# Sliding-window attention and gated MLP: where the x^T of batches 3 to 7 is transposed, and when batch 3's scores start

## The chip, the cores and the metric

The kernel runs on one core of one Trainium2 chip. The metric is the device time of one execution in microseconds (us). Executions of one and the same kernel scatter by about one per cent here, so medians of several runs are given, and effects of less than a microsecond are read from the lengths of single stages in the profile.

## The reference, cut to what matters

```python
# attention: q, k, v are (8 batches, 8 heads, 576 positions, 64)
scores = (q @ k^T) / 8;  masked to 0 <= i - j < 64
attn   = softmax(scores);  out = attn @ v
# x: (4608 tokens, 512), the heads of a token side by side
h = x @ w_in                      # (4608, 2048)
g = h * clip(h + 3, 0, 6) / 6
return (g @ w_out)                # (4608, 512), float32
```

## The kernel before

The MLP goes in nine stages of 512 tokens (0 to 8). A stage has two halves: `s1` makes 16 chunks of the hidden layer, each of four 128x512 matmuls, and `s2` makes four output tiles in four quarters each, again four matmuls per quarter. So a stage has 128 large matmuls on TensorE (PE). The attention of a later batch is woven between them as *pieces*: stage 1 computes batch 2, stage 2 batch 3, and so on to stage 6 with batch 7. `p1` lists the pieces after each chunk of `s1`, `p2` those after each quarter of `s2`.

A batch has four pairs of heads. For each pair, `SS` makes the scores (PE), the exponentials (ScalarE, ACT) and the mask (VectorE, DVE); `N_` makes PV on PE and normalizes on DVE; then the result has to be transposed, to become x^T, the right operand of the next stages. That is done either by PE and a copy (`X_`), or by a DMA transpose (`xt_dma`), which the sync engine's queue (SP) issues.

```python
def xt_pe(bt, g, tr):                       # X_ calls it
    opg = opgs.pop((bt.b, g))
    for qb in range(KB):                    # KB = 5
        nc.tensor.transpose(out=tr[:, qb * P : (qb + 1) * P], in_=..., identity=ident[:])
    return lambda: acopy(out=xT[:, g, bt.b * S : (bt.b + 1) * S], in_=tr[:, 0:S])

def xt_dma(bt, g):
    ...
    nc.sync.dma_start_transpose(out=xT[:, g, t0 : t0 + SP].rearrange(...), in_=opg[:]...)

def pieces(bt):
    ...                                     # batch 2: all by X_
    p1 = {10: [f(SS, 0)], 14: [f(SS, 1)]}   # batches 3 to 7
    p2 = {
        0: [f(SS, 2)], 1: [f(N_, 0)], 3: [f(SS, 3), f(xt_dma, 0)], 4: [f(N_, 1)],
        6: [f(xt_dma, 1)], 7: [f(N_, 2)], 9: [f(xt_dma, 2)], 10: [f(N_, 3)], 12: [f(X_, 3)],
    }
    return p1, p2
...
for T in range(1, NTB):
    p1, p2 = pieces(nxt)
    b = T + 2
    if b < B:
        sts, _ = load_for_dma(b)            # 15 loads of q, k, v on SP
        nxt = Batch(b)
        p1.setdefault(12 if T == 1 else 6, []).append(...cast_for_dma(sts))   # POOL
        p2.setdefault(6 if T == 1 else 12, []).append(...transpose_by_dma())  # QT, KT, on SP
    stage_(T, None, p1, p2)
```

The same SP queue thus carries, in program order, the loads of the batch after next, its QT and KT transposes (SBUF to SBUF), the x^T transposes of the current batch, and the output tiles.

The softmax here doesn't subtract the row's maximum and nothing guards it: scores larger than these inputs give would overflow.

Of the kernel before, what the change touches and what calls it, by code (L numbers as in the profile page):

```python
# [24 lines left out]
def kernel(  # L25
# [98 lines left out]
    def load_for_dma(b):  # L124
        sts, ins = [], []
        for n, src in (("qst", q), ("kst", k), ("vst", v)):
            t = stage.tile([P, KB, H, D], F32, name=n, tag=n)
            ins += load_blocks(t, src, b, range(KB), SR if src is v else 0)
            sts.append(t)
        return tuple(sts), ins  # L130
# [446 lines left out]
    bt, st = Batch(0), stage0  # L577
# [77 lines left out]
    bt, st = Batch(1), st1  # L655
# [56 lines left out]
    def stage_(T, bt, pieces1, pieces2):  # L712
        if T == 1:
            m = s1(1, ((0, 1), (2,)))
            run(m, 1)
            X_(Batch(1), NG - 1)
            run(m, 1)
        else:
            m = s1(T)
        for i in range(NFC):  # L720
            run(m, 1)
            for f in pieces1.get(i, ()):
                f()
        m = s2(T, BY_BLOCK)
        for i in range(16):
            run(m, 1)
            for f in pieces2.get(i, ()):
                f()

    def pieces(bt):  # L730
        if bt is None:
            return {}, {}
        f = lambda fn, *a: lambda: fn(bt, *a)
        p1, p2 = {}, {}
        if bt.b == 2:
            return p1, {
                0: [f(SS, 0)], 1: [f(SS, 1)], 3: [f(N_, 0), f(SS, 2)], 5: [f(X_, 0)],
                6: [f(N_, 1), f(SS, 3)], 8: [f(X_, 1)], 9: [f(N_, 2)], 11: [f(X_, 2)],
                12: [f(N_, 3)], 14: [f(X_, 3)],
            }  # L740
        p1 = {10: [f(SS, 0)], 14: [f(SS, 1)]}
        p2 = {
            0: [f(SS, 2)], 1: [f(N_, 0)], 3: [f(SS, 3), f(xt_dma, 0)], 4: [f(N_, 1)],
            6: [f(xt_dma, 1)], 7: [f(N_, 2)], 9: [f(xt_dma, 2)], 10: [f(N_, 3)], 12: [f(X_, 3)],
        }
        return p1, p2

# [6 lines left out]
    nxt, pend = bt2, None  # L754
# [3 lines that stand above are left out]
        nxt = None  # L758
        if b < B:
            sts, _ = load_for_dma(b)  # L760
            nxt = Batch(b)
            p1.setdefault(12 if T == 1 else 6, []).append(
                lambda bt=nxt, sts=sts: bt.cast_for_dma(sts)
            )
            p2.setdefault(6 if T == 1 else 12, []).append(lambda bt=nxt: bt.transpose_by_dma())
        stage_(T, None, p1, p2)


# [28 lines left out]
```

## Time and profile before

| what | kernel before |
|---|---|
| median of the first runs | 319.6 us |
| span of the profile | 317.6 us |
| PE busy | 300.8 us (95%) |
| ACT, DVE busy | 56%, 55% |
| stage 2 with stage 3 | 67.3 us |
| stages 4, 5, 6 | 32.03, 32.04, 32.04 us |
| stage 7 (no attention in it) | 27.6 us |

A stage is measured here from the first large matmul of its `s1` that the profile shows to that of the next stage. Some matmul records are missing from some profiles. If the first matmul of stage 3 is one of them, its row counts 7 and not 8. Stage 2 then reads too long, and stage 3 reads 0.22 us too short; sums over both are right. The first lines of the profile page of the kernel before:

```profile
span 317.6 us, 5604 instructions
PE 300.8 (95%) x2131; PEld 149.5 (47%) x2167; DVE 173.9 (55%) x331; ACT 177.9 (56%) x265; POOL 85.7 (27%) x131
```

PE is the engine that bounds the kernel. In the steady stages there is no idle time on it to speak of. The busy times by stretch of the kernel before, for stages 2 and 3 together and then for stages 4 and 5 (columns: stretch, length, busy time of each engine with its instruction count, granted PE clock, DMA share, GB/s):

```profile
95.06:162.37 67.31, 63.72 (x467) 31.74 (x475) 38.98 (x72) 38.58 (x58) 25.50 (x34) 1.00 1.17 220
162.37:194.40 32.03, 31.82 (x234) 15.85 (x237) 19.72 (x36) 19.17 (x29) 9.71 (x13) 1.00 1.04 203
194.40:226.44 32.04, 31.83 (x235) 15.87 (x237) 19.93 (x36) 19.17 (x29) 10.27 (x13) 1.00 1.02 201
```

Stages 4 to 6 have 0.2 us of idle time each; stages 2 and 3 have 3.6 us in 67.3. The waits of PE from stage 2 to the end of stage 6, in the kernel before (engine, line, what it waited for: total us, times, longest):

```profile
PE st L347 <- DMA KT<-kn: 2.0, 1, 2.0
PE st L466 <- DMA xT<-opg: 1.0, 1, 1.0
```

The PE timeline of the kernel before shows where these are: the first scores of batch 3 wait for KT, and stage 3 waits for x^T after its first matmuls. (The last bracket is the idle time before the instruction and what ended it.)

```profile
103.69 1.03 PE L466 MATMUL hT<-xT,win 128*128 128x512 bf16 x4
106.69 0.51 PE L347 MATMUL st<-QT,KT 64*128 64x192 bf16 x10 [1.97 <-DMA KT<-kn]
...
126.26 0.44 PE L407 MATMUL hT<-ident,opg 128*128 128x128 bf16 x5
126.54 2.54 PE L503 MATMUL acc<-wout,gT 128*128 128x512 bf16 x11
129.13 0.59 PE L466 MATMUL st<-xT,win 128*128 128x512 bf16 x2
130.77 1.46 PE L466 MATMUL st<-xT,win 128*128 128x512 bf16 x6 [1.04 <-DMA xT<-opg]
```

The row with `ident` is one x^T by PE: five transposes, and 0.28 us later the next matmul issues. The SP queue of the kernel before in the same stage (start, duration of issuing, what):

```profile
102.24 2.75 SPq L266 DMA_TRANSPOSE KT<-kn  x1
...
106.64 4.92 SPq L94 DMA_DIRECT2D qst<-in_q_dram  x5
111.61 5.39 SPq L94 DMA_DIRECT2D kst<-in_k_dram  x5
117.10 6.92 SPq L94 DMA_DIRECT2D vst<-in_v_dram  x5
...
124.78 2.60 SPq L418 DMA_TRANSPOSE xT<-opg  x2
127.48 0.53 SPq L512 DMA_DIRECT2D out_dram<-osb  x1
128.11 1.24 SPq L418 DMA_TRANSPOSE xT<-opg  x1
```

The lines left out are output tiles; the queue has no gap over 0.1 us from 102 to 129 us. The x^T transposes stand behind fifteen loads.

### The profile page before, as it was taken

The numbers are of one execution on the slowest core, as the hardware profiler recorded it, in microseconds if no ns is written. First come the engines' busy times: TensorE is split into PE (matmuls) and PEld (weight loads), VectorE is DVE, ScalarE is ACT, GpSimd is POOL, SyncE is SP. The second block draws the span as 40 slices with busy tenths as digits, with TensorE's granted clock in tenths as the row PEclk, the third lists the DMA queues.
The fourth block names the chain that finished last, engine by engine and source line by source line (L and its number), as shares of the span: only waits on it lengthen the run. The fifth ranks groups of instructions, "written<-read, shape, count | busy, mean of one in ns | idle before, by whom it ended". The sixth has DMA issues, their size and how long they took to land.

```text
span 317.6 us, 5604 instructions
## 1 busy us (share of the span) xinstructions
PE 300.8 (95%) x2131; PEld 149.5 (47%) x2167; DVE 173.9 (55%) x331; ACT 177.9 (56%) x265; POOL 85.7 (27%) x131
## 2 busy tenths in 40 slices
PE   8989799999999799899999999999999999999995
PEld 3454345544554355344544554445444544444442
DVE  4658643476636665277527853785378438406700
ACT  2748753387637771487258725872587347417711
POOL 5741805363045143305610650065000000000000
PEclk9999999999999999999999999999999999999999
DMA  8999999999799999999999998999800630010011
GB/s 211 237 173 253 238 199 205 204 184 248 158 208 209 270 215 205 191 254 204 195 257 210 207 184 208 211 201 185 204 34 2 122 75 0 28 73 33 0 68 66
DMA packets 150843, 52.64 MB, mean 166 GB/s; under 512 B 138272, under 2 KB 146464, under 8 KB 150816
## 3 DMA queue, kind: packets, MB, share of 16 engines
q1 hardware_dynamic: 146000, 46.77, 72.7%
q0 software_dynamic: 4544, 5.24, 9.5%
q8 instruction: 17, 0.28, 0.4%
q10 hardware_dynamic: 272, 0.26, 0.2%
q14 instruction: 10, 0.08, 0.1%
HBM read 36.70 MB, written 9.44 MB: 145 GB/s over the span
## 4 chain that ended last, share of the span: by engine, by line
PE 63%; DMA 21%; SPq 8%; POOL 3%; issue 2%; DVE 1%; ACT 1%; POOLq 0%
PE o L503 15%; PE acc L503 14%; PE hT L466 14%; PE acc L466 5%; PE o L466 5%; SPq L94 5%; DMA vst<-in_v_dram 4%; DMA kst<-in_k_dram 4%; DMA KT<-kn 4%; DMA qst<-in_q_dram 3%; PE st L466 3%; PE st L347 3%; DMA wout<-in_moe_w_out_dram 3%; DMA win<-in_moe_w_in_dram 3%; PE hT L377 1%
## 5 line engine op out<-in xcount | busy, mean ns | idle before, releaser
L466 PEld LDWEIGHTS <-win 128*128 128x128 bf16 x576 | 55.3, 98 | 67.2 <-issue 2.3
L503 PEld LDWEIGHTS <-gT 128*128 128x128 bf16 x576 | 52.9, 98 | 57.5 <-issue 0.6
L503 PE MATMUL o<-wout,gT 128*128 128x512 bf16 x274 | 67.5, 379 | 1.5 <-DMA wout<-in_moe_w_out_dram 0.7
L503 PE MATMUL acc<-wout,gT 128*128 128x512 bf16 x278 | 67.1, 379 | 0.7 <-issue 0.3
L466 PE MATMUL hT<-xT,win 128*128 128x512 bf16 x266 | 65.7, 379 | 0.3
L355 ACT ACTIVATE pT<-st 128x768 bf16<-128x768 f32 x64 | 48.9, 813 | 10.8 <-PE st L347 10.7
L473 ACT ACTIVATE t<-hT,half 128x512 bf16<-128x512 f32 x68 | 46.7, 690 | 9.6 <-PE hT L466 9.2
L474 DVE SCALAR_TENSOR_TENSOR gT<-t,hT 128x512 bf16<-128x512 bf16 x68 | 46.4, 685 | 9.4 <-ACT t L473 9.1
L474 DVE SCALAR_TENSOR_TENSOR gT<-t,st 128x512 bf16<-128x512 bf16 (+1 forms) x26 | 19.7, 768 | 52.9 <-ACT t L473 52.9
L365 DVE TENSOR_TENSOR pT<-pT,mask 128x1536 bf16<-128x1536 bf16 x28 | 28.1, 1004 | 23.0 <-ACT pT L355 23.0
L509 ACT COPY osb<-o 128x512 f32<-128x512 f32 x18 | 10.6, 586 | 46.2 <-PE o L503 46.2
L252 POOL CAST qn<-qst 128x512 bf16<-128x512 f32 x24 | 16.1, 712 | 74.1 <-DMA qst<-in_q_dram 59.7
L509 ACT COPY osb<-acc 128x512 f32<-128x512 f32 x18 | 10.6, 587 | 35.7 <-PE acc L503 33.7
L466 PE MATMUL st<-xT,win 128*128 128x512 bf16 x117 | 28.2, 379 | 1.7 <-DMA xT<-opg 1.0
L397 DVE TENSOR_TENSOR opg<-hT,rec 128x320 bf16<-128x320 f32 x56 | 27.5, 492 | 1.9
L466 PE MATMUL acc<-xT,win 128*128 128x512 bf16 x91 | 23.6, 379 | 0.1
L466 PE MATMUL o<-xT,win 128*128 128x512 bf16 x90 | 23.5, 379 | 0.1
L473 ACT ACTIVATE t<-st,half 128x512 bf16<-128x512 f32 (+1 forms) x26 | 19.4, 752 | 7.2 <-PE st L466 7.1
L377 PEld LDWEIGHTS <-pT 128*128 128x128 bf16 x256 | 17.8, 97 | 9.1 <-issue 1.4
L347 PE MATMUL st<-QT,KT 64*128 64x192 bf16 (+2 forms) x320 | 17.9, 229 | 4.2 <-DMA KT<-kn 2.4
L394 DVE RECIPROCAL rec<-hT 128x5 f32<-128x5 f32 x56 | 10.5, 188 | 20.0 <-PE hT L386 19.9
L243 POOL CAST V<-vst 128x512 bf16<-128x512 f32 (+1 forms) x14 | 16.4, 1168 | 17.4 <-DMA vst<-in_v_dram 17.0
(76 smaller groups left out, 269.2 us busy)
## 6 DMA issues: line engine op xcount, KB each, us to landing
out_dram<-osb SPq DMA_DIRECT2D x32, 256.0 KB, 2.4
qst<-in_q_dram SPq DMA_DIRECT2D x28, 256.0 KB, 4.7
kst<-in_k_dram SPq DMA_DIRECT2D x27, 256.0 KB, 5.4
vst<-in_v_dram SPq DMA_DIRECT2D x24, 256.0 KB, 5.1
vst<-in_v_dram SPq DMA_DIRECT2D x24, 128.0 KB, 4.1
win<-in_moe_w_in_dram POOLq DMA_DIRECT2D x4, 512.0 KB, 7.6
wout<-in_moe_w_out_dram POOLq DMA_DIRECT2D x4, 512.0 KB, 8.8
qst<-in_q_dram SPq DMA_DIRECT2D x2, 512.0 KB, 6.1
```

What stands on the lines that cost most here:

```text
L243: copy(out=self.V[:, 0 : KB - 1, h0:h1, 0:D], in_=vst[:, 0 : KB - 1, h0:h1, :])
L252: pcopy(out=n[:, g, 0 : KB - 1, :, :].rearrange("p k h d -> p k (h d)"), in_=s[:, 0 : KB - 1, 2 * g : 2 * g + 2, :].rearrange("p k h d -> ...
L347: nc.tensor.matmul(st[:, h, o0 : o0 + n], lhsT=bt.KT[h * D : (h + 1) * D, g, k0 : k0 + P], rhs=bt.QT[h * D : (h + 1) * D, g, q0 : q0 + n], ...
L355: nc.scalar.activation(out=pT[:, :, 2 * u : 2 * u + 2, 0:QW], in_=st[:, :, 0:w].rearrange("p h (k w) -> p h k w", k=2), func=EXP, scale=scale,
L365: nc.vector.tensor_tensor(out=pT[:, :, :, 0:QW], in0=pT[:, :, :, 0:QW], in1=mask[:].rearrange("p (h k) w -> p h k w", h=2), op=MULT,)
L377: nc.tensor.matmul(ob, lhsT=pT[:, h, qb, 0:P], rhs=V[:, qb, 2 * g + h, :], start=True, stop=(qb == 0),)
L397: nc.vector.tensor_tensor(out=opgs[bt.b, g][:, :, h, :], in0=ov[:, :, 0:D], in1=rec[:].unsqueeze(2).to_broadcast([P, KB, D]), op=MULT,)
L466: nc.tensor.matmul(hT, lhsT=win16[:, g, fc * P : (fc + 1) * P], rhs=xT[:, g, t0 : t0 + TB], start=(g == 0), stop=(g == NG - 1),)
L473: nc.scalar.activation(out=t1[:], in_=hT, func=RELU, bias=half[:], scale=1.0 / 6.0)
L474: nc.vector.scalar_tensor_tensor(out=out, in0=t1[:], scalar=1.0, in1=hT, op0=MIN, op1=MULT,)
L503: nc.tensor.matmul(accs[ts], lhsT=gT[:, fc, ts * P : (ts + 1) * P], rhs=wout16[:, fc, :], start=(fc == 0), stop=(fc == NFC - 1),)
L509: nc.scalar.copy(out=osb[:], in_=accs[ts])
```

## The change

Its intent: batch 3 asks for KT later and takes all its x^T by PE, since SP is late in stage 2; from batch 4 on, the fourth x^T goes by DMA too, which takes the transposes off PE, and PV is moved up so that the last DMA is in time. The QT/KT transposes of batch 4 move from quarter 12 of stage 2 to quarter 6.

```diff
+        if bt.b == 3:
+            return {13: [f(SS, 0)]}, {
+                0: [f(SS, 1)], 3: [f(N_, 0), f(SS, 2)], 5: [f(X_, 0)], 6: [f(N_, 1), f(SS, 3)],
+                8: [f(X_, 1)], 9: [f(N_, 2)], 11: [f(X_, 2)], 12: [f(N_, 3)], 14: [f(X_, 3)],
+            }
-        p1 = {10: [f(SS, 0)], 14: [f(SS, 1)]}
+        p1 = {10: [f(SS, 0)], 13: [f(SS, 1)]}
         p2 = {
-            0: [f(SS, 2)], 1: [f(N_, 0)], 3: [f(SS, 3), f(xt_dma, 0)], 4: [f(N_, 1)],
-            6: [f(xt_dma, 1)], 7: [f(N_, 2)], 9: [f(xt_dma, 2)], 10: [f(N_, 3)], 12: [f(X_, 3)],
+            0: [f(SS, 2)], 1: [f(N_, 0)], 2: [f(SS, 3)], 3: [f(N_, 1), f(xt_dma, 0)],
+            5: [f(xt_dma, 1)], 6: [f(N_, 2)], 8: [f(N_, 3), f(xt_dma, 2)], 10: [f(xt_dma, 3)],
         }
...
-            p2.setdefault(6 if T == 1 else 12, []).append(lambda bt=nxt: bt.transpose_by_dma())
+            p2.setdefault(6 if T < 3 else 12, []).append(lambda bt=nxt: bt.transpose_by_dma())
```

## The prediction

> **What bounds the kernel now.** TensorE: PE is busy 300.8 us of 317.6 (95%), ACT 56%, DVE 55%; granted clock 1.00 throughout. In the timeline 128x512 matmuls issue every 0.216 us, so a pure stage of 128 takes 27.6 us (stages 7, 8). An attention stage adds four pairs of scores (0.44 us each), eight PV heads (0.25 us each) and one x^T by PE (0.28 us for five transposes): about 31.7; stages 4 to 6 take 32.0 to 32.2. The idle time is in stage 2 (batch 3): the waits view has PE on KT<-kn for 2.4 us, the longest 1.97 us at 104.7 to 106.7 (pair 0 of batch 3, asked after chunk 10); and 1.04 us on xT<-opg at the start of stage 3. There SP's queue is late: the loads of batch 4 occupy it to 124.0, and the third x^T transpose issues at 128.1, landing 2.6 us later.
>
> **What the change does.**
> 1. Batch 3's scores start three chunks (2.6 us) later. KT landed at 106.6; PE will ask at about 107.2. Saves 1.97 us, with half a microsecond of slack.
> 2. Batch 3's x^T all by PE: +15 transposes, 3 x 0.28 = +0.84 us. The last copy is placed as in stage 1, after which stage 2 began without a wait. Removes the 1.04 us wait.
> 3. Batch 4's QT/KT transposes move ahead in SP's queue, so stage 3's loads start near 132 rather than 137 us. Off PE's path; slack only.
> 4. Batches 4 to 7: the fourth x^T by DMA. PE 4 x -0.28 = -1.12 us. SP gets one 1.24 us issue more per stage. In stage 5 its loads end at 214.8 and its QT transpose starts at 223.9, so it fits. Last x^T issued near 221.4, landing (median 2.9 us) near 224.3, before the next stage at 226.1: no wait.
> 5. PV one or two quarters earlier: worth nothing to PE, needed for 4. Its price: PV of pair 1 asks for its PSUM bank 2.8 us after PV of pair 0, before which DVE must mask pair 2 and do four small instructions. With the mask at 0.96 us that just fits; in stages 4 and 5 one took 1.36 us as a POOL cast started beside it. The Trainium skill ("SBUF — State Buffer", on the shared port pair) says that DVE and GpSimd exclude each other there; the trace agrees in that instruction. I allow 0 to 0.35 us a stage, +0.4 in all.
>
> The skill ("TensorE: Matmul & The Clock Gate", Part 4) gives about 275 ns for a 128x128 PE transpose in a kernel; here five in a row hold PE up only 0.28 us together, which I use. So net PE work falls only 0.28 us.
>
> **Sum.** -1.97 - 1.04 + 0.84 - 1.12 + 0.4 = -2.9 us: 319.6 becomes 316.7 (range 315.5 to 318.2), 0.9% faster, all on PE's chain, most of it in stage 2 and at stage 3's start. Chances: faster by over 2% 0.02, within 2% 0.96, slower 0.02.
>
> **What would show it.** 1: no wait over 0.3 us on KT in stage 2. 2: none on xT at stage 3's start, which comes near 127.9 instead of 129.1. 3: stage 3's loads begin by 133. 4: stages 3 to 6 take 31.7 to 32.0 us; 16 x^T transposes by DMA, the fourth landing over 1 us before the next stage. 5: small idle times of PE before PV of pair 1, on DVE.
>
> **What would make it wrong.** KT landing later than before (DMA engines are nearly full in stage 2); the fourth transpose queued behind late loads on SP, giving 1 us or more of wait at four stage starts (then 319 to 320); PV stalls in every stage, larger than allowed.

## The result

The changed kernel took 316.08 us (median; 314.71 to 316.42 over four runs; a fifth took 316.84), the kernel before 319.67 us in the same rounds. The ratio is 0.9887 (95% interval 0.9849 to 0.9926): 1.1% faster. Ratios here and below are the mean time of one kernel's fast runs over that of the other's of the same rounds, so they are not quite the ratio of the medians quoted. Two repeats in later sessions gave 0.9892 and 0.9889.

The span of the changed kernel's profile is 4.7 us shorter, but 1.3 us of that lie before stage 2 (which began at 93.75 instead of 95.06 us), where the change touches nothing. Its repeats began stage 2 at 96.10 and 95.06 us, so this part is scatter. What belongs to the change is the stretch from stage 2 to the end of stage 6: 163.42 us before, 160.00 after (160.26 and 161.11 in the two later profiles of the changed kernel; the last of them has a wait of 0.76 us, see below). The page of the changed kernel and the same three stretches:

```profile
span 312.9 us, 5589 instructions
PE 298.8 (96%) x2126; PEld 149.0 (48%) x2162; DVE 174.5 (56%) x331; ACT 177.2 (57%) x264; POOL 86.1 (28%) x131
```

```profile
93.75:158.37 64.62, 64.04 (x476) 32.54 (x484) 39.38 (x72) 39.94 (x60) 25.77 (x34) 1.00 1.15 220
158.37:190.13 31.76, 31.55 (x230) 15.60 (x233) 19.94 (x36) 18.52 (x28) 10.25 (x13) 1.00 1.03 214
190.13:222.00 31.87, 31.66 (x230) 15.64 (x233) 19.78 (x36) 18.51 (x28) 10.32 (x13) 1.00 1.11 207
```

Stages 2 and 3 became 2.7 us shorter although PE is busy 0.3 us longer there, and stages 4 to 6 became 0.27, 0.17 and 0.29 us shorter with PE less busy by the same amount. The PE timeline of the changed kernel, at the places where the kernel before waited:

```profile
105.94 0.51 PE L347 MATMUL st<-QT,KT 64*128 64x192 bf16 x10
...
126.84 1.67 PE L466 MATMUL st<-xT,win 128*128 128x512 bf16 x7
```

Neither row has a bracket: both waits are gone. And the SP queue of the changed kernel in stages 2 and 3:

```profile
100.87 2.80 SPq L266 DMA_TRANSPOSE KT<-kn  x1
...
123.11 3.54 SPq L266 DMA_TRANSPOSE QT<-qn  x1
126.75 3.74 SPq L266 DMA_TRANSPOSE KT<-kn  x1
...
132.14 4.95 SPq L94 DMA_DIRECT2D qst<-in_q_dram  x5
...
150.28 2.60 SPq L418 DMA_TRANSPOSE xT<-opg  x2
...
153.60 2.56 SPq L418 DMA_TRANSPOSE xT<-opg  x2
```

The loads of stage 3 begin at 132.1 us instead of 137.0 (38.4 us after the start of stage 2 instead of 41.9), and all four x^T of batch 4 are issued by 156.2 us. The last one starts at 154.9 and lands 2.6 us later, at 157.5, before stage 4 begins at 158.4.

### The profile page after: what moved, and what is told of

It is laid out like the page before. It is cut to its first block, busy times and chain, and to the rows that moved or that the text cites. A ratio compares the mean times of both kernels' runs of the same rounds, so it can differ in the third digit from the quotient of the medians.

```text
span 312.9 us, 5589 instructions
## 1 busy us (share of the span) xinstructions
PE 298.8 (96%) x2126; PEld 149.0 (48%) x2162; DVE 174.5 (56%) x331; ACT 177.2 (57%) x264; POOL 86.1 (28%) x131
## 4 chain that ended last, share of the span: by engine, by line
PE 88%; ACT 3%; DMA 3%; SPq 2%; DVE 1%; issue 1%; POOL 1%
PE o L503 20%; PE acc L503 19%; PE hT L466 18%; PE st L466 8%; PE acc L466 6%; PE o L466 6%; PE st L347 4%; PE hT L377 2%; PE hT L382 2%; DMA qst<-in_q_dram 1%; PE hT L407 1%; DMA vst<-in_v_dram 1%; ACT pT L355 1%; DVE gT L474 1%; SPq L82 1%
## 5 line engine op out<-in xcount | busy, mean ns | idle before, releaser
L503 PE MATMUL acc<-wout,gT 128*128 128x512 bf16 x275 | 66.1, 379 | 0.8 <-issue 0.2
L466 PE MATMUL hT<-xT,win 128*128 128x512 bf16 x267 | 64.9, 379 | 0.3
```

What stands on the lines that cost most here:

```text
L466: nc.tensor.matmul(hT, lhsT=win16[:, g, fc * P : (fc + 1) * P], rhs=xT[:, g, t0 : t0 + TB], start=(g == 0), stop=(g == NG - 1),)
L503: nc.tensor.matmul(accs[ts], lhsT=gT[:, fc, ts * P : (ts + 1) * P], rhs=wout16[:, fc, :], start=(fc == 0), stop=(fc == NFC - 1),)
```

## The experiments

The sum in the prediction treats the two waits as separate items. A rival reading is that they stand one behind the other on SP: the x^T transposes come when the loads are through, so if PE arrives earlier because one wait is gone, it only waits longer at the next. To tell them apart, the two parts of batch 3 were tried alone. All four kernels of this first set have the new schedule for batches 4 to 7, and ran on one chip.

| kernel | scores of batch 3 | x^T of batch 3 | median us | ratio to before (95%) | stages 2+3, us | waits of PE in stages 2 to 6 |
|---|---|---|---|---|---|---|
| only_b4on | after chunk 10 | 3 DMA, 1 PE | 318.23 | 0.9947 (0.9915 to 0.9979) | 69.09 | KT 3.0 |
| b3_by_dma | after chunk 13 | 3 DMA, 1 PE | 318.31 | 0.9954 (0.9921 to 0.9986) | 67.08 | xT 2.8 |
| scores_early | after chunk 10 | PE | 318.89 | 0.9962 (0.9928 to 0.9997) | 66.88 | KT 2.1 |
| after_again | after chunk 13 | PE | 316.77 | 0.9892 (0.9856 to 0.9927) | 64.80 | none |

The kernel before had a median of 320.21 us in these rounds.

### Batches 4 to 7 alone: only_b4on

```diff
# against the changed kernel: batch 3 and the place of QT/KT as in the kernel before
-            return {13: [f(SS, 0)]}, { ...all by X_... }
+            p1 = {10: [f(SS, 0)], 14: [f(SS, 1)]}
+            p2 = { ...as in the kernel before, xt_dma 0 to 2, X_ 3... }
```

> Batch 3 as in the kernel before, batches 4 to 7 as in the change. My sum: only the four x^T transposes of 0.28 us leave TensorE, so about 1.0 us off before (ratio about 0.997); stages 4 to 6 take about 31.8 us instead of 32.0; both waits of batch 3 are still there: about 2 us on KT in stage 2 (a little more or less with the moment the transpose lands) and about 1 us on xT at the start of stage 3. Rival: most of the gain of the whole change comes from these batches (ratio 0.991 or less).

Measured: the ratio is 0.9947, about where the sum puts it (0.997 is inside the interval), and stages 5 and 6 take 31.76 and 31.75 us; stage 4 takes 32.06, for a reason given under step 5 below. The profiled execution was slower than the others of this kernel (319.57 us, clock 0.995 over the span) and shows something that was not expected. The wait on KT was 2.96 us instead of 1.97, and the matmuls after it ran at half speed. The PE timeline of only_b4on:

```profile
106.40 0.51 PE L347 MATMUL st<-QT,KT 64*128 64x192 bf16 x10 [2.96 <-DMA KT<-kn]
106.84 1.54 PE L466 MATMUL hT<-xT,win 128*128 128x512 bf16 x4
108.18 1.91 PE L466 MATMUL o<-xT,win 128*128 128x512 bf16 x4
109.88 1.41 PE L466 MATMUL acc<-xT,win 128*128 128x512 bf16 x4
```

Four matmuls that take 0.86 us from one row to the next elsewhere took 1.70 us from 108.18 to 109.88. The busy times of only_b4on in the stretches 106 to 111 and 111 to 116 us confirm that it is the clock (the third number from the end):

```profile
106.00:111.00 5.00, 4.60 (x22) 1.98 (x23) 1.71 (x3) 2.89 (x4) 0.00 (x0) 0.66 1.14 271
111.00:116.00 5.00, 5.00 (x46) 2.45 (x45) 3.60 (x5) 4.50 (x7) 1.79 (x2) 1.00 1.35 211
```

Stage 2 lasted 37.2 us in this execution. PE reached stage 3 so late, at 130.95 us, that x^T had landed, and the second wait does not appear. This is taken up again below.

### The late scores alone: b3_by_dma

```diff
# against the changed kernel (QT/KT of batch 4 also back after quarter 12)
             return {13: [f(SS, 0)]}, {
-                0: [f(SS, 1)], 3: [f(N_, 0), f(SS, 2)], 5: [f(X_, 0)], 6: [f(N_, 1), f(SS, 3)],
-                8: [f(X_, 1)], 9: [f(N_, 2)], 11: [f(X_, 2)], 12: [f(N_, 3)], 14: [f(X_, 3)],
+                0: [f(SS, 1)], 3: [f(N_, 0), f(SS, 2)], 5: [f(xt_dma, 0)], 6: [f(N_, 1), f(SS, 3), f(xt_dma, 1)],
+                9: [f(N_, 2)], 10: [f(xt_dma, 2)], 12: [f(N_, 3)], 14: [f(X_, 3)],
```

> As only_b4on, but batch 3's scores three chunks later; its x^T still by DMA for three pairs, QT/KT of batch 4 in the old place. Independent-waits theory (as my prediction adds them up): the KT wait of about 2 us goes and the xT wait stays at about 1 us, so 2 us faster than only_b4on. Series theory: the start of stage 3 is set by the SP queue (loads of batch 4 until about 29 us after the start of stage 2, then the x^T transposes in a row), which does not move when TensorE arrives earlier; the KT wait goes and the xT wait grows to 2.5 to 3.5 us; the same time as only_b4on within 0.5 us.

Measured: the wait on KT is gone, and the wait on x^T grew from 1.04 to 2.8 us. The time is that of only_b4on. The PE timeline of b3_by_dma at the start of stage 3:

```profile
128.04 0.38 PE L466 MATMUL st<-xT,win 128*128 128x512 bf16 x1 [1.51 <-DMA xT<-opg]
128.58 0.38 PE L466 MATMUL st<-xT,win 128*128 128x512 bf16 x1 [0.16 <-DMA xT<-opg]
130.08 1.46 PE L466 MATMUL st<-xT,win 128*128 128x512 bf16 x6 [1.12 <-DMA xT<-opg]
```

PE now waits for each of the three transposes in turn. Its third x^T was issued at 127.30 us, 33.0 us after the start of stage 2, as in the kernel before (128.11, 33.1 us after). The stretch of stages 2 and 3 is 67.08 us against 67.31 before, and 0.28 of that is the fourth x^T of batch 4 that left PE in stage 3. So the late scores alone gained nothing: the wait of 1.97 us came back at the next place where PE meets the SP queue. The series theory holds, and the items of the sum are not independent. No run put the x^T transposes ahead of the loads in SP's queue, which would be another way to have them earlier.

### The x^T by PE alone: scores_early

```diff
-            return {13: [f(SS, 0)]}, {
+            return {10: [f(SS, 0)]}, {
```

> The changed kernel, but batch 3's first scores after chunk 10 as before; its x^T by PE. Both theories: a wait on KT of about 2 us comes back in stage 2, no wait on xT at the start of stage 3, about 2 us slower than the changed kernel. If the KT wait were not the reason, it would be as fast as the changed kernel.

Measured: a wait on KT of 2.08 us in stage 2, no wait on x^T, and 318.89 us against 316.77 of the changed kernel on the same chip. Stage 2 is 35.0 us, 2.1 us more than in the changed kernel on the same chip (32.87 in after_again). The PE timeline of scores_early:

```profile
105.54 0.51 PE L347 MATMUL st<-QT,KT 64*128 64x192 bf16 x10 [2.08 <-DMA KT<-kn]
```

So the wait is worth its full length once nothing from SP stands behind it.

### The changed kernel again: after_again

> The changed kernel again, as the comparison for the three others on this chip. Ratio to before about 0.989 (3 to 4 us less). Its stage 2 begins within 0.5 us of where the kernel before has it if the 1.3 us that its first profile began stage 2 earlier was chance; if it begins 1.3 us earlier again, the change does something to the stages before it that I do not know of.

Measured: 316.77 us, ratio 0.9892. Stage 2 began at 96.10 us, 1.0 us later than in the kernel before (0.5 was expected at most) and not earlier again, so the early start in the first profile was chance. This execution had a wait on KT of 0.84 us in stage 1 (batch 2) and none in stage 2.

### Batch 3 alone: only_b3

```diff
-        p1 = {10: [f(SS, 0)], 13: [f(SS, 1)]}
-        p2 = { ...four xt_dma... }
+        p1 = {10: [f(SS, 0)], 14: [f(SS, 1)]}
+        p2 = { ...as in the kernel before... }
```

> Batch 3 as in the change (late scores, x^T by PE, QT/KT of batch 4 earlier), batches 4 to 7 as before. My sum: -1.97 (KT) -1.04 (xT) +0.84 (15 transposes) = about 2.2 us off before, ratio about 0.993; stages 4 to 6 take 32.0 us as before. Rival: under 1 us.

This and the next three ran on another chip of the same kind, where the kernel before had a median of 320.31 us (318.75 to 323.33) and the scatter was larger. Measured: 318.89 us, ratio 0.9946 (0.9896 to 0.9995). Stage 2 reads 33.08 us, and stages 3 to 6 32.03, 32.04, 32.03 and 32.03 us: from stage 2 to the end of stage 6 161.21 us, 2.2 less than before, as the sum says.

### The fourth x^T back on PE: fourth_pe

```diff
-            ...10: [f(xt_dma, 3)],
+            ...10: [f(X_, 3)],
```

> The changed kernel, but the fourth x^T of batches 4 to 7 on TensorE again, in the same place (PV still moved up). My sum: 4 x 0.28 = about 1.1 us slower than the changed kernel, plus what TensorE waits for DVE before the transposes (they come two quarters after PV of pair 3: none expected). Stages 4 to 6 about 32.1 us.

Measured: 317.66 us (median of five fast runs and one slow one of 322.93), ratio of the fast runs 0.9913. Stages 4 to 6 took 32.03, 32.32 and 32.03 us; from stage 2 to the end of stage 6 161.28 us, 1.3 us more than in the changed kernel (160.00; 160.26 in its repeat, on another chip). The sum said 1.1. Stage 5 is the one that is too long, and not by chance: it is taken up under step 5 below. There is no wait longer than 0.2 us in these stages.

### PV in its old place: pv_stays

```diff
-        p1 = {10: [f(SS, 0)], 13: [f(SS, 1)]}
+        p1 = {10: [f(SS, 0)], 14: [f(SS, 1)]}
         p2 = {
-            0: [f(SS, 2)], 1: [f(N_, 0)], 2: [f(SS, 3)], 3: [f(N_, 1), f(xt_dma, 0)],
-            5: [f(xt_dma, 1)], 6: [f(N_, 2)], 8: [f(N_, 3), f(xt_dma, 2)], 10: [f(xt_dma, 3)],
+            0: [f(SS, 2)], 1: [f(N_, 0)], 3: [f(SS, 3), f(xt_dma, 0)], 4: [f(N_, 1)],
+            6: [f(xt_dma, 1)], 7: [f(N_, 2)], 9: [f(xt_dma, 2)], 10: [f(N_, 3)], 12: [f(xt_dma, 3)],
```

> The changed kernel, but with the old places for scores, PV and x^T in batches 4 to 7: only the fourth x^T, after quarter 12, goes by DMA instead of PE. If moving PV is needed (step 5 of my prediction): the last x^T transpose is issued at about 29.0 us of the stage, lands about 31.8, and TensorE, which wants it at about 32.4, waits 0 to 1 us at four stage starts: up to 4 us slower than the changed kernel. If it isn't needed: the same time within 0.5 us and no wait on xT.

Measured: 317.33 us, ratio 0.9914 (0.9862 to 0.9966); from stage 2 to the end of stage 6 160.37 us, against 160.00 and 160.26 of the changed kernel. There is no wait on x^T. The SP queue of pv_stays at the end of stage 3, and PE there:

```profile
159.39 1.24 SPq L418 DMA_TRANSPOSE xT<-opg  x1
```

```profile
161.61 1.89 PE L466 MATMUL st<-xT,win 128*128 128x512 bf16 x7
```

The last x^T, issued at 159.39, lands 2.6 us later at 162.0. Stage 4 starts at 161.61, and its fourth matmul, the first that reads this pair, comes three matmuls of 0.216 us later, at 162.3. It is in time by some 0.3 us, and by 0.2 to 0.3 us at the next three stage starts. So in the execution profiled the move of PV was not needed; it only widens the margin.

### QT/KT in its old place: qkt_late

```diff
-            p2.setdefault(6 if T < 3 else 12, []).append(lambda bt=nxt: bt.transpose_by_dma())
+            p2.setdefault(6 if T == 1 else 12, []).append(lambda bt=nxt: bt.transpose_by_dma())
```

> The changed kernel, but QT/KT of batch 4 transposed after quarter 12 of stage 2 as before, and not after quarter 6. Step 3 of my prediction (slack only): the same time within 0.5 us. SP issues the QT transpose only 1 to 2 us later, since the loads hold its queue to about 28.7 us of the stage in both. Rival: the move is what keeps stage 3 free of a KT wait: then a wait on KT in stage 3 of 1 us or more.

Measured: 316.39 us, ratio 0.9878 (0.9835 to 0.9922); from stage 2 to the end of stage 6 160.13 us. No wait on KT in stage 3. This part of the change is worth nothing by itself, as expected.

### A longer wait on purpose: scores_at_7

The half-speed stretch of only_b4on asked for a test. Here batch 3 asks for KT three chunks earlier still.

```diff
-            return {13: [f(SS, 0)]}, {
+            return {7: [f(SS, 0)]}, {
```

> The changed kernel, but batch 3's first scores already after chunk 7: TensorE asks for KT about 5 us before it lands, and idles some 4.7 us. If only the idle time counts: 2.6 us more than with the scores after chunk 10, so about 4.6 us slower than the changed kernel (about 321), and the matmuls after the wait still issue every 0.216 us. If a long idle time also lowers the granted clock, as the profile of only_b4on suggests (clock 0.80 between 103 and 110 us, matmuls at 0.43 us after an idle time of 2.96 us): matmuls at about 0.43 us for some 4 us after the wait, clock in that window well under 1, and about 2 us more (about 323).

Measured: 322.9 us against 316.34 of the changed kernel in the same rounds, 6.6 us more, as the second reading expects. The PE timeline of scores_at_7 and its busy times in the stretches 106 to 111 and 111 to 113 us:

```profile
106.87 0.82 PE L347 MATMUL st<-QT,KT 64*128 64x192 bf16 x10 [4.54 <-DMA KT<-kn]
107.62 1.89 PE L466 MATMUL o<-xT,win 128*128 128x512 bf16 x4
...
111.01 2.79 PE L466 MATMUL hT<-xT,win 128*128 128x512 bf16 x8
```

```profile
106.00:111.00 5.00, 4.13 (x18) 1.77 (x19) 1.65 (x2) 2.20 (x3) 0.00 (x0) 0.50 1.07 271
111.00:113.00 2.00, 2.00 (x7) 0.77 (x6) 0.69 (x1) 0.73 (x2) 0.00 (x0) 0.55 1.33 220
```

The clock is 0.50 after the wait, and 1.00 again from 113 us. From 106.87 to 113.63 us, where the next row starts, PE issued one set of scores and sixteen large matmuls, which take 0.44 + 16 x 0.216 = 3.90 us at full clock; they took 6.76. The wait of 4.54 us thus cost a further 2.9 us. Every execution of this kernel has a mean clock of 0.995 or less, but this alone says little: so have nine of the eleven executions of the kernel before in the same rounds. In the profiled execution stage 3 was also about 1 us longer than elsewhere (32.84 us), with 0.7 us of waits on DVE before PV.

The length of a single wait is not all that matters to the clock. The profile of pv_stays has two stretches of half clock of 3.4 us, at 20.0 and 40.5 us, and no wait of PE over 1.0 us in the few microseconds before them. The busy times around the first:

```profile
16.50:20.00 3.50, 1.95 (x43) 1.63 (x41) 2.41 (x8) 1.45 (x3) 2.97 (x7) 1.00 1.20 167
20.00:23.40 3.40, 3.18 (x15) 1.47 (x13) 2.01 (x8) 0.64 (x1) 0.29 (x1) 0.50 1.22 201
```

What set the clock there no run tells.

### One chunk more: scores_at_14, with after_third

```diff
-            return {13: [f(SS, 0)]}, {
+            return {14: [f(SS, 0)]}, {
```

> The changed kernel, but batch 3's first scores one chunk later still (after chunk 14), as a try at more slack for KT (half a microsecond in the changed kernel). If KT is late in some executions of the changed kernel, this one gains up to 0.5 us there; else the same within 0.3 us. The masks come one chunk later and could hold PV of pair 0 up: then a new idle time of TensorE before it.

> The changed kernel once more, for comparison on this chip: about 3.5 us less than before, no wait on KT or on xT in stages 2 and 3.

Measured: scores_at_14 316.28 us (ratio 0.9891), after_third 316.34 us (ratio 0.9889): the same. But the profile of after_third has the wait that the changed kernel was to be free of. The PE timeline of after_third in stage 2:

```profile
108.07 0.51 PE L347 MATMUL st<-QT,KT 64*128 64x192 bf16 x10 [0.76 <-DMA KT<-kn]
```

In that execution KT was issued at 103.64 us and landed 13.0 us after the start of stage 2, while the scores ask at 12.2. In the two other profiles of the changed kernel it landed 11.5 and 11.8 us after it. after_again, which had waited 0.84 us for KT in stage 1, had no wait in stage 2; after_third had none in stage 1 and 0.76 us in stage 2. One could see the series reading in that, but it is not shown: the first profile of the changed kernel, only_b3, fourth_pe and pv_stays waited for KT in neither stage. The extra chunk of scores_at_14 shows no wait in stage 2 (32.87 us), nor an idle time before PV, but no gain in the median either; in its profile KT landed 11.7 us after the start of stage 2, so the extra slack was not put to use. No version tried beats the changed kernel clearly.

## Why the prediction was right

The prediction said 316.7 us (315.5 to 318.2); it came to 316.08 us. Point by point:

- **What bounds the kernel** was read correctly. From stage 2 to the end of stage 6, 3.4 us went, where the sum said 2.9. The half microsecond is two errors of the same sign: the waits were taken too short and the price of step 5 too high (both below).
- **Steps 1 and 2 (late scores, x^T of batch 3 by PE).** Both waits are gone in the first profile, and stage 2 takes 32.87 us instead of 34.07. Stages 2 and 3 together lost 2.69 us. The sum of the same items there is -1.97 - 1.04 + 0.84 - 0.28 = -2.45. The waits view counts from the end of the matmul before, which is later than the moment at which the next one could issue. Counted by issue (0.216 us after the last matmul), PE lost 2.13 and 1.21 us, and the sum is -2.78. What the prediction did not see is that the first two items are one gain and not two. "Saves 1.97 us" is true only together with step 2; alone it saved nothing (b3_by_dma), since SP delivers x^T no earlier. The x^T by PE alone left the 2 us on KT (scores_early).
- **The slack of half a microsecond at KT** was 0.7 us in the first profile (KT landed 4.4 us after 100.87, PE asked at 105.94) and was not enough in one profiled execution of three (0.76 us of wait in after_third). Called "half a microsecond of slack" it was right in size, but it is smaller than the scatter of the landing, 11.5 to 13.0 us after the stage's start in these three. Over all thirteen profiles it is 10.7 to 13.0 us, and in two of them, only_b4on and after_third, KT landed after the 12.2 us at which the changed kernel asks. That the first profile showed no wait was partly luck.
- **Step 3 (QT/KT earlier, slack only).** Right: qkt_late is as fast. The loads of stage 3 began at 132.1 us, as said, but 1.3 us of that is the early start of this execution.
- **Step 4 (fourth x^T by DMA, -0.28 us a stage).** Right: stages 4 and 6 are 0.27 and 0.29 us shorter, and putting it back on PE costs 1.0 to 1.3 us over four stages (fourth_pe). The landing was 0.8 us before stage 4 and not "over 1 us". Of the twelve landings in the three profiles of the changed kernel seven came less than 1 us before the next stage, the closest 0.07 us (after_third). No wait followed, but part of that margin is luck too.
- **Step 5 (PV moved: "needed for 4", price 0.4 us).** This step failed. The move wasn't needed for the time measured: pv_stays has no wait on x^T, with 0.3 us to spare. And the price was too high: in the changed kernel stages 4 and 6 have none of it, and stage 5 is 0.11 us longer than its neighbours (31.87 against 31.76 and 31.75; 0.2 us in after_again). The estimate took for granted that the mask of pair 2 falls beside a POOL cast and takes 1.36 us, as in the kernel before. In the changed kernel it took 0.96 us in stages 3 to 6, and the mask of pair 1 was the slow one (1.33 us in stage 5). The mechanism itself exists: in stage 4 of only_b4on, where the mask of pair 2 did take 1.36 us, the second head of PV of pair 1 started only at 183.34 us, just after DVE had freed its bank (at 183.28), some 0.15 us late. fourth_pe, which has the same places for PV, paid most in one stage: in its stage 5 the mask of pair 2 took 1.34 us, the second heads of PV of pairs 0 and 1 came 0.12 and 0.16 us late, and the stage is 0.29 us longer than its neighbours. So the range of 0 to 0.35 us a stage was right, and the sum of 0.4 too high for what these executions drew.
- **PE transposes.** Five in a row were set at 0.28 us and not at five times the 275 ns that the Trainium skill ("TensorE: Matmul & The Clock Gate", Part 4) gives for one. fourth_pe bears that out within the open ends of step 5; one lasts 219 ns in the trace, so they overlap.

## What to carry to other kernels

Two waits of the busiest engine on one and the same DMA queue are not two gains: ask for each one whether the queue would deliver the next thing any earlier, and if not, change both or neither. Choose the place of a request by the scatter of the landing, not by one trace; half a microsecond of slack did not cover 1.5 us of scatter. And a long wait can cost more than its length: in the two profiles with waits of 2.96 and 4.54 us the clock was halved behind them, in those with 1.97 and 2.08 us it was not.

## What the Trainium skill lacked or had wrong

- "TensorE: Matmul & The Clock Gate": the table of rules says that there should be no idle gaps over about 3 us between bursts of matmuls, and Part 1 describes a free-running window of about 3.4 us. The runs agree for the waits tested: an idle time of 2.96 us was followed by half clock in the execution profiled (0.66 over the next 5 us), 4.54 us by a clock of 0.50, and 1.97 and 2.08 us by full clock. What the runs add is the price in a dense kernel: 2.9 us more after a wait of 4.54 us. They also show half clock without such a gap: twice 3.4 us in pv_stays, with no wait over 1.0 us before it.
- The same page, Part 4, gives about 275 ns for one PE transpose of 128x128 in a kernel, but not the rate of several in a row: here five hold the next matmul up by 0.28 us, while each lasts 219 ns in the trace.
- "VectorE: DVE Perf Modes", section "The three transpose paths", gives 1309 ns for a 128x128 transpose by DMA, and this section has nothing on the queue that issues it: here an x^T transpose of five such blocks took SP about 1.24 us to issue and landed 2.6 to 5.4 us after that began (median 3.0; the first profile of the changed kernel), and those of QT and KT, of twenty blocks, took 2.4 to 4.9 us to issue over all profiles.
- "DMA: Bandwidth & Descriptors", section "Issuing engines are not separate DMA queues", calls the sequencer's time to initiate a DMA "usually small relative to the DMA itself". Here fifteen loads held SP for 17.4 us of a 34 us stage (106.64 to 124.02 us in stage 2), and the x^T transposes behind them could not start. Whether issuing itself or a full queue below it takes that time, no run tells.
